# Expert feed-forward: the first product with its weights stationary and its tokens moving

## The chip, the cores and the metric

The kernel runs on one core of a Trainium2 chip. The metric is the device time of one execution in microseconds; less is better. The inputs are the seeded ones of the reference, and the whole computation is one launch.

## The reference, cut to what matters

Three parts follow each other. `_attn_ref` and `_moe_ref` give, for each of 8 × 576 tokens, a row `x` of 512 numbers. The change lies in the third part, a mixture of eight experts in which each token goes to one expert only (weights `w1` 8 × 512 × 1024, `w2` 8 × 1024 × 512):

```
def _moe2_ref(x, w_gate, w_local, w1, w2):
    ...
            e = ...                                  # the expert of this token
            p = np.exp(ls); p /= p.sum() + 1e-09     # softmax of the gate
            h = np.maximum(x[b, s] @ w1[e], 0.0)     # first product, 512 -> 1024
            out[b, s] = p[e] * (h @ w2[e])           # second product, 1024 -> 512
```

## The kernel before, in words

**Number format.** Every large product is done in f16 with each operand split in two: a high part and what the rounding left, the low part. `PASS = ((0, 0), (0, 1), (1, 0))` names the three partial products that are kept (high × high, high × low, low × high). So each product of a 128-row slice costs three matmuls.

**Stages.** Attention and the dense mix (`Mix.mm1` at L733 and `Mix.mm2` at L753) fill the first 1048 us of the profiled execution. Routing then sorts the tokens by expert into blocks of 128 tokens: 9 early blocks, and 34 from the second half of the routing. 41 of the 43 blocks are always computed; the last two stand behind a branch. The expert stage runs over these blocks, one after the other.

**One block of the expert stage.** `load_x(b)` gathers the 128 token rows (high and low part, 128 × 1024) by an indirect DMA on POOL's queue (L1069) and turns them by a DMA transpose on SP's queue (L1073) into `xt[b]`, 128 × 8 × 128: the features on the partitions, slices 0 to 3 the high part, 4 to 7 the low one. `load_w1` and `load_w2` (both through `weights`, L1083) fetch the split weights of the block's expert from DRAM into one of three buffers each, in four slices of 0.5 MB, on SP's queue; the DMA is skipped if the buffer holds that expert already (`cond=c`). `e1(b)` is the first product, for two groups `fg` of 512 hidden columns: 12 matmuls (4 slices of features × 3 passes) with the tokens stationary (128 × 128) and 512 columns of `w1` moving, into one PSUM bank `hp` (L1099). The result has the tokens on the partitions. ScalarE writes the high part of relu(hp) (L1106), VectorE the low part (L1107), both into the buffer `h` (tile `hb`, two buffers). The second product needs the hidden index on the partitions, so a DMA transpose on SP's queue (L1108) turns `h` into `ht` (tile `hx`, two buffers), one for each `fg`. `e2(b)` is the second product: 24 matmuls with `ht` stationary and 512 columns of `w2` moving (L1118), then a scaling by ScalarE (L1124) and an indirect DMA of the rows to the output on POOL's queue (L1125).

**Order.** The program text of the loop is `load_x(b + 3)`, `e1(b + 1)`, `e2(b)`. The weight loads for block b + 3 (`w1`) and b + 2 (`w2`) are issued inside the loops of `e1` and `e2`, one slice at a time, and `tick()` steps a list of background generators: in the first blocks these are the second half of the routing. A scheduler orders the instructions of each engine at build time by priority and its own estimate of when operands are there; on the chip each engine then takes its instructions in that fixed order. SP does no arithmetic: its queue carries, for each block, eight weight loads, two transposes of `h` and one transpose of `x`, in order.

Of the kernel before, what the change touches and what calls it, by code (L numbers as in the profile page):

```python
# [9 lines left out]
F16 = mybir.dt.float16  # L10
I32 = mybir.dt.int32
AF = mybir.ActivationFunctionType
ALU = mybir.AluOpType
# [12 lines left out]
RB = 3  # L26
# [135 lines left out]
PASS = ((0, 0), (0, 1), (1, 0))  # L162
# [16 lines left out]
def _build(tc, nc, ctx, A, stop):  # L179
# [517 lines left out]
    def tick(n=1.0):  # L697
        for it in list(bg):
            if it[0] is ew and phase[0] < EWS:
                continue  # L700
            it[1] += it[2] * n
            while it[1] >= 1.0:
                it[1] -= 1.0
                try:
                    next(it[0])
                except StopIteration:
                    bg.remove(it)
                    break
# [338 lines left out]
    M = {}  # L1047
# [14 lines left out]
    w1b, w2b = [], []  # L1062
    xg, xt, regs, hb = {}, {}, {}, {}
# [11 lines left out]
    def weights(b, dst, src, k0, k1):  # L1075

        if b not in regs:
            regs[b] = (nc.sync.value_load(ebi[0:1, 0, b:b + 1], min_val=0, max_val=NE - 1),
                       nc.sync.value_load(ebi[0:1, 1, b:b + 1], min_val=0, max_val=1))
        e, c = regs[b]  # L1080
        flat = dst[b % RB].rearrange("p c a n -> p (c a n)")
        cols = slice(2048 * k0, 2048 * k1)
        nc.sync.dma_start(flat[:, cols], src[bass.ds(e, 1), :, cols].rearrange("o p x -> p (o x)"), cond=c)  # L1083

    def load_w1(b, k0=0, k1=4):
        weights(b, w1b, WS1, k0, k1)

    def load_w2(b, k0=0, k1=4):
        weights(b, w2b, WS2, k0, k1)

    def e1(b, nxt=None):
        h = M["q"].tile([128, 2, 1024], F16, tag="hb", name=f"hb{b}", bufs=2)
        ht = M["q"].tile([128, 2, 8, 128], F16, tag="hx", name=f"hx{b}", bufs=2)
        for fg in range(2):
            hp = (psM, psO)[fg].tile([128, 512], F32, tag="ho"[fg], name=f"ehp{b}_{fg}")
            n = 0
            for c in range(4):
                for (x, y) in PASS:
                    nc.tensor.matmul(hp, xt[b][:, 4 * x + c], w1b[b % RB][:, 2 * c + fg, y],  # L1099
                                     start=n == 0, stop=n == 11)  # L1100
                    n += 1
                if c % 2 == 0 and nxt is not None:
                    load_w1(nxt, 2 * fg + c // 2, 2 * fg + c // 2 + 1)
                if c < 3:
                    tick()
            nc.scalar.activation(h[:, fg, :512], hp, AF.Relu)  # L1106
            nc.vector.scalar_tensor_tensor(h[:, fg, 512:], hp, 0.0, h[:, fg, :512], ALU.max, ALU.subtract)  # L1107
            nc.sync.dma_start_transpose(out=ht[:, fg], in_=h[:, fg])  # L1108
            tick()
        hb[b] = ht  # L1110

    def e2(b, nxt=None):
        h = hb.pop(b)
        op = psO.tile([128, 512], F32, tag="o", name=f"eo{b}")
        n = 0
        for f in range(8):
            for (x, y) in PASS:
                nc.tensor.matmul(op, h[:, f // 4, 4 * x + f % 4], w2b[b % RB][:, f, y], start=n == 0, stop=n == 23)  # L1118
                n += 1
            if f % 2 == 0 and nxt is not None:  # L1120
                load_w2(nxt, f // 2, f // 2 + 1)
            tick()
        ys = wp.tile([128, 512], F32, tag="U", name=f"ys{b}", bufs=8)
        nc.scalar.activation(ys, op, AF.Copy, scale=scl[:, b:b + 1])  # L1124
        nc.gpsimd.indirect_dma_start(out=A["out"], out_offset=bass.IndirectOffsetOnAxis(ap=sidx[:, b:b + 1], axis=0),  # L1125
                                     in_=ys, in_offset=None, bounds_check=NB * S - 1, oob_is_err=False)
# [61 lines left out]
    bg.append([r1, 0.0, R1_RATE])  # L1188
    load_w2(1)
    e1(0, 2)  # L1190
    last_sure = NBLK - NRARE

# [3 lines left out]
    for b in range(last_sure):  # L1196
        if b + RB == NEARLY:
            drain(r1)
        if sure(b + AHEAD) is not None:
            load_x(b + AHEAD)  # L1200
        if b + 1 < last_sure:
            e1(b + 1, sure(b + RB))
        e2(b, sure(b + RB - 1))
# [4 lines left out]
    def rare(b):  # L1208
        if b == NBLK:
            return  # L1210
        with tc.If(nused > b - NEARLY):
            load_x(b)
            load_w1(b)
            load_w2(b)
            e1(b)
            e2(b)
            rare(b + 1)
# [19 lines left out]
```

## Time and profile before

| | |
|---|---|
| median of 3 runs | 1526.61 us (1518.05 to 1538.52) |
| the profiled execution | 1531.01 us, span 1529.1 us, mean granted clock 0.966 |
| PE busy in the span | 1396.3 us (91%) |
| DVE, ACT, POOL busy | 769.7, 482.2, 335.8 us |
| expert stage, first e1 matmul to the end | 1048.6 to 1529.1 us |
| matmuls of e1 (L1099) and of e2 (L1118) | 984 each, 24 a block for 41 blocks |

PE is TensorE's matmuls and PEld its weight loads, which run beside them. A matmul's duration in the profile is its latency; matmuls overlap, so the time from one to the next is shorter than the duration. The granted clock is a share of 2.4 GHz; 1.0 is the upper level and 0.5 the lower one, 1.2 GHz. SPq is SP's queue, which issues DMAs.

### The profile page before, as it was taken

To read this page: it belongs to the slowest core of one execution; us is meant where nothing else is said; L and a number is where in the kernel's file an instruction comes from. 1 tells how busy PE (TensorE), PEld (TensorE's weight loads), DVE (VectorE), ACT (ScalarE), POOL (GpSimd) and SP (SyncE) were. 2 spreads that over 40 slices of the span, in tenths; PEclk is the share of its full clock that TensorE was granted. 3 is DMA by queue.
4 is the path that set the end of the run, shared out by engine and by line. 5 is a ranking of instruction groups with operands and counts; after the bars stand their busy time and mean duration, and the time that the engine had idled before them with its cause. 6 is when DMAs were issued, how large, how long until landed. Compare 5 with 4: busy or idle time off the path is not lost. (4 is left out here: it accounts for less than half of the span.)

```text
span 1529.1 us, 23161 instructions
## 1 busy us (share of the span) xinstructions
PE 1396.3 (91%) x8436; PEld 690.6 (45%) x8436; DVE 769.7 (50%) x1583; ACT 482.2 (32%) x892; POOL 335.8 (22%) x332
## 2 busy tenths in 40 slices
PE   3487899999999999999999999999899899989996
PEld 2233444534564454454444456454444344434442
DVE  6779967567555756666766765523611111111110
ACT  5355544344333434434434333111111111111111
POOL 4346423203200420320321220010112112111211
PEclk6698999999999999999999999999999999999998
DMA  8374465376466546547547355345968969897696
GB/s 266 80 228 144 146 180 164 97 219 171 122 155 166 186 120 200 151 134 208 148 131 208 104 139 152 96 160 168 288 133 191 236 139 226 201 324 147 131 206 161
DMA packets 319733, 260.82 MB, mean 171 GB/s; under 512 B 254784, under 2 KB 266176, under 8 KB 318977
## 3 DMA queue, kind: packets, MB, share of 16 engines
q1 hardware_dynamic: 313056, 239.13, 59.1%
q0 software_dynamic: 6560, 20.19, 4.4%
q8 instruction: 67, 1.10, 0.3%
q14 instruction: 50, 0.40, 0.1%
HBM read 267.38 MB, written 53.74 MB: 210 GB/s over the span
## 5 line engine op out<-in xcount | busy, mean ns | idle before, releaser
L753 PE MATMUL acc<-w2h,ht 128*128 128x512 f16 x1728 | 414.0, 382 | 0.8 <-DVE ul L761 0.8
L733 PE MATMUL hp<-ut,w1h 128*128 128x512 f16 x1536 | 376.5, 386 | 8.1 <-DMA ut<-unh 3.6
L733 PEld LDWEIGHTS <-w1h 128*128 128x128 f16 x1920 | 184.5, 99 | 194.9 <-issue 25.2
L753 PEld LDWEIGHTS <-ht 128*128 128x128 f16 x1728 | 166.6, 98 | 186.9 <-issue 10.4
L1118 PE MATMUL eo<-w2b,hx 128*128 128x512 f16 x984 | 229.7, 383 | 14.6 <-DMA hx<-hb 14.1
L1107 DVE SCALAR_TENSOR_TENSOR hb<-ehp,hb 128x512 f16<-128x512 f32 x82 | 56.7, 691 | 358.5 <-ACT hb L1106 326.4
L1099 PE MATMUL ehp<-w1b,xgt 128*128 128x512 f16 x984 | 229.5, 381 | 5.2 <-DMA w1b<-WS 3.4
L741 DVE SCALAR_TENSOR_TENSOR ht<-hp,ht 128x512 f16<-128x512 f32 (+1 forms) x160 | 101.4, 634 | 167.1 <-ACT ht L740 167.0
L1118 PEld LDWEIGHTS <-hx 128*128 128x128 f16 x984 | 96.0, 99 | 135.4 <-DMA hx<-hb 20.6
L1099 PEld LDWEIGHTS <-xgt 128*128 128x128 f16 x984 | 95.8, 98 | 121.6 <-issue 5.7
L260 ACT ACTIVATE so<-se 128x512 f16<-128x512 f32 x128 | 79.5, 628 | 181.9 <-DMA WS<-so 159.7
L740 ACT ACTIVATE ht<-hp 128x512 f16<-128x512 f32 (+1 forms) x160 | 87.4, 547 | 132.9 <-PE hp L733 127.4
L1125 POOL DMA_INDIRECT out<-ys,sidx x41 | 41.8, 1020 | 337.2 <-ACT ys L1124 332.4
L1124 ACT ACTIVATE ys<-eo,scl 128x512 f32<-128x512 f32 x41 | 28.2, 687 | 272.7 <-PE eo L1118 272.6
L346 POOL TENSOR_TENSOR qh<-q,qh 128x1420 f16<-128x1420 f32 x15 | 44.1, 2937 | 280.3 <-ACT qh L345 280.2
L261 DVE SCALAR_TENSOR_TENSOR so<-se,so 128x512 f16<-128x512 f32 x128 | 100.0, 790 | 10.3 <-ACT so L260 10.3
L1069 POOL DMA_INDIRECT xg<-XS,gidx x41 | 42.5, 1035 | 182.7 <-DVE sidx L1025 103.9
L1106 ACT ACTIVATE hb<-ehp 128x512 f16<-128x512 f32 x82 | 48.9, 597 | 105.6 <-PE ehp L1099 103.2
L370 PE MATMUL s<-k,p 64*32 64x288 f32 x256 | 24.8, 488 | 27.0 <-DVE ru L642 12.3
L733 PE MATMUL hp<-utr,w1h 128*128 128x256 f16 x384 | 47.1, 272 | 0.0
L557 PE MATMUL bp<-cst,eh 128*128 128x289 f16 (+1 forms) x192 | 33.0, 312 | 14.1 <-DVE g L472 5.9
L688 POOL TENSOR_TENSOR unh<-un,unh 128x512 f16<-128x512 f32 x32 | 38.6, 1214 | 30.6 <-ACT unh L687 30.6
(290 smaller groups left out, 1394.0 us busy)
## 6 DMA issues: line engine op xcount, KB each, us to landing
w1b<-WS SPq DMA_DIRECT2D x156, 512.0 KB
w2b<-WS SPq DMA_DIRECT2D x156, 512.0 KB
se<-in_w SPq DMA_DIRECT2D x64, 512.0 KB
WS<-so SPq DMA_DIRECT2D x128, 256.0 KB
sw<-in_wc SPq DMA_DIRECT2D x32, 512.0 KB
q<-in_qd SPq DMA_DIRECT2D x16, 710.0 KB
v<-in_vd SPq DMA_DIRECT2D x16, 640.0 KB
k<-in_kd SPq DMA_DIRECT2D x16, 576.0 KB
```

Source lines behind the costliest of these rows:

```text
L260: nc.scalar.activation(dst_hi, src, AF.Copy, scale=scale)
L261: nc.vector.scalar_tensor_tensor(dst_lo, src, scale, dst_hi, ALU.mult, ALU.subtract)
L346: nc.gpsimd.tensor_tensor(qh[:, 1], qt, qh[:, 0], op=ALU.subtract)
L733: nc.tensor.matmul(hp[:, :ntok], w1h[:, f, c, x], ut[:, 4 * y + c, :ntok], start=n == 0, stop=n == 11)
L740: nc.scalar.activation(ht[:, 0, :ntok], hp[:, :ntok], AF.Relu)
L741: pace[0] = nc.vector.scalar_tensor_tensor(ht[:, 1, :ntok], hp[:, :ntok], 0.0, ht[:, 0, :ntok], ALU.max, ALU.subtract).ins
L753: nc.tensor.matmul(self.acc[j], ht[:, x, 128 * j:128 * j + 128], w2h[:, f, y], start=f == 0 and n == 0, stop=f == 15 and n == 2)
L1069: nc.gpsimd.indirect_dma_start(out=g_, out_offset=None, in_=XS[0:rows], in_offset=bass.IndirectOffsetOnAxis(ap=gidx[:, b:b + 1], axis=0), ...
L1099: nc.tensor.matmul(hp, xt[b][:, 4 * x + c], w1b[b % RB][:, 2 * c + fg, y], start=n == 0, stop=n == 11)
L1106: nc.scalar.activation(h[:, fg, :512], hp, AF.Relu)
L1107: nc.vector.scalar_tensor_tensor(h[:, fg, 512:], hp, 0.0, h[:, fg, :512], ALU.max, ALU.subtract)
L1118: nc.tensor.matmul(op, h[:, f // 4, 4 * x + f % 4], w2b[b % RB][:, f, y], start=n == 0, stop=n == 23)
```

## The change

`e1` is turned around: the weights become the stationary operand, 128 hidden columns at a time, and the 128 tokens of the block move. A group `fg` is now four column blocks `f` of 12 matmuls each, 48 matmuls of 128 moving columns in place of 12 of 512; all four write their own 128 columns of the same PSUM bank. The result already has the hidden index on the partitions, so ScalarE and VectorE write the two parts straight into `ht`, and the DMA transposes of `h` and the buffer `hb` go. `hx` gets a third buffer. The weight loads and the calls of `tick()` stand at the same places of the loop, now counted by `f` in place of `c`. `e2` reads the same numbers from the new layout.

```diff
     def e1(b, nxt=None):
-        h = M["q"].tile([128, 2, 1024], F16, tag="hb", name=f"hb{b}", bufs=2)
-        ht = M["q"].tile([128, 2, 8, 128], F16, tag="hx", name=f"hx{b}", bufs=2)
+
+        ht = M["q"].tile([128, 2, 2, 512], F16, tag="hx", name=f"hx{b}", bufs=3)
         for fg in range(2):
             hp = (psM, psO)[fg].tile([128, 512], F32, tag="ho"[fg], name=f"ehp{b}_{fg}")
-            n = 0
-            for c in range(4):
-                for (x, y) in PASS:
-                    nc.tensor.matmul(hp, xt[b][:, 4 * x + c], w1b[b % RB][:, 2 * c + fg, y],
-                                     start=n == 0, stop=n == 11)
-                    n += 1
-                if c % 2 == 0 and nxt is not None:
-                    load_w1(nxt, 2 * fg + c // 2, 2 * fg + c // 2 + 1)
-                if c < 3:
+            for f in range(4):
+                n = 0
+                cols = slice(128 * f, 128 * f + 128)
+                for c in range(4):
+                    for (x, y) in PASS:
+                        nc.tensor.matmul(hp[:, cols], w1b[b % RB][:, 2 * c + fg, x, cols], xt[b][:, 4 * y + c],
+                                         start=n == 0, stop=n == 11, skip_group_check=True)
+                        n += 1
+                if f % 2 == 0 and nxt is not None:
+                    load_w1(nxt, 2 * fg + f // 2, 2 * fg + f // 2 + 1)
+                if f < 3:
                     tick()
-            nc.scalar.activation(h[:, fg, :512], hp, AF.Relu)
-            nc.vector.scalar_tensor_tensor(h[:, fg, 512:], hp, 0.0, h[:, fg, :512], ALU.max, ALU.subtract)
-            nc.sync.dma_start_transpose(out=ht[:, fg], in_=h[:, fg])
+            nc.scalar.activation(ht[:, fg, 0], hp, AF.Relu)
+            nc.vector.scalar_tensor_tensor(ht[:, fg, 1], hp, 0.0, ht[:, fg, 0], ALU.max, ALU.subtract)
             tick()
         hb[b] = ht
...
         for f in range(8):
             for (x, y) in PASS:
-                nc.tensor.matmul(op, h[:, f // 4, 4 * x + f % 4], w2b[b % RB][:, f, y], start=n == 0, stop=n == 23)
+                nc.tensor.matmul(op, h[:, f // 4, x, 128 * (f % 4):128 * (f % 4) + 128], w2b[b % RB][:, f, y],
+                                 start=n == 0, stop=n == 23)
                 n += 1
```

## Rows read from the trace of the kernel before

**Rows 1.** Windows of the expert stage: start:end, length, busy per engine, PEclk, DMA share, GB/s
```profile
1048.60:1112.00 63.40, 55.48 (x326) 29.19 (x325) 39.79 (x126) 10.99 (x19) 8.60 (x8) 0.97 0.99 283
1112.00:1340.00 228.00, 221.22 (x1016) 99.21 (x1015) 29.90 (x45) 39.42 (x64) 42.99 (x42) 0.99 0.82 188
1340.00:1406.00 66.00, 59.47 (x263) 25.28 (x262) 7.10 (x11) 9.21 (x15) 10.23 (x10) 0.97 0.93 243
1406.00:1490.00 84.00, 84.00 (x390) 38.04 (x389) 11.07 (x16) 14.73 (x24) 14.30 (x14) 1.00 0.75 164
1490.00:1518.00 28.00, 24.79 (x112) 10.52 (x110) 2.77 (x4) 4.37 (x7) 2.95 (x3) 1.00 0.95 221
```

**Rows 2.** Waits, 1048 to 1519 us: who waited for whom, us, times, longest
```profile
PE eo L1118 <- DMA hx<-hb: 14.1, 10, 2.7
...
PE ehp L1099 <- DMA w1b<-WS: 3.4, 4, 2.1
...
PE ehp L1099 <- DMA xgt<-xg: 1.8, 3, 1.4
```

**Rows 3.** Timeline of PE around stalls: start, length, instructions, [idle before]
```profile
1213.90 4.27 PE L1118 MATMUL eo<-w2b,hx 128*128 128x512 f16 x12 [2.69 <-DMA hx<-hb]
...
1351.73 0.81 PE L1099 MATMUL ehp<-w1b,xgt 128*128 128x512 f16 x3 [2.09 <-DMA w1b<-WS]
...
1354.33 4.03 PE L1118 MATMUL eo<-w2b,hx 128*128 128x512 f16 x12
```

**Rows 4.** Timeline of PE, one undisturbed block apart
```profile
1246.49 2.75 PE L1118 MATMUL eo<-w2b,hx 128*128 128x512 f16 x12
...
1256.85 2.75 PE L1118 MATMUL eo<-w2b,hx 128*128 128x512 f16 x12
```

**Rows 5.** Instructions of four lines: duration in ns, min/median/max, first to last start
```profile
L1099 PE MATMUL ehp<-w1b,xgt x984: 376/379/634, 1048.6 to 1506.7; 128*128 128x512 f16 x197
...
L733 PE MATMUL hp<-utr,w1h x384: 269/273/273, 423.6 to 953.7; 128*128 128x256 f16 x192
...
L485 PE MATMUL s<-pth,qh x540: 189/193/261, 29.1 to 847.0; 128*128 128x64 f16 x180
...
L429 PE MATMUL pps<-vhl,et x450: 216/219/316, 19.1 to 832.5; 128*64 128x128 f16 x150
```

**Rows 6.** Timeline of PE: runs of short matmuls in earlier stages
```profile
427.45 1.47 PE L733 MATMUL hp<-utr,w1h 128*128 128x256 f16 x12
...
846.33 0.83 PE L485 MATMUL s<-pth,qh 128*128 128x64 f16 x23
...
831.78 0.89 PE L429 MATMUL pps<-vhl,et 128*64 128x128 f16 x26
...
833.27 0.17 PE L770 MATMUL lp<-wgh,xt 128*128 128x18 f16 x1
...
833.45 0.17 PE L772 MATMUL lp<-wgh,xt 128*128 128x9 f16 x1
```

**Rows 7.** SP's issue of the two transposes of a block, ns min/median/max
```profile
L1108 SPq DMA_TRANSPOSE hx<-hb x82: 971/1257/3911, 1056.3 to 1508.5; - x82
...
L1073 SPq DMA_TRANSPOSE xgt<-xg x41: 962/1242/6377, 1023.3 to 1481.2; - x41
```

**Rows 8.** Waits of SP's own queue, 1048 to 1519 us
```profile
SPq L1108 <- DVE hb L1107: 21.0, 21, 2.4
```

**Rows 9.** Groups of instructions by line: count | busy us, mean ns | idle before
```profile
L1107 DVE SCALAR_TENSOR_TENSOR hb<-ehp,hb 128x512 f16<-128x512 f32 x82 | 56.7, 691 | 358.5 <-ACT hb L1106 326.4 <-DMA hx<-hb 14.2 <-DMA xgt<-xg 7.1
L1106 ACT ACTIVATE hb<-ehp 128x512 f16<-128x512 f32 x82 | 48.9, 597 | 105.6 <-PE ehp L1099 103.2 <-issue 2.0 <-DMA hx<-hb 0.4
```

**Rows 10.** Page: span and instructions; DMA queue of instruction blocks (packets, MB, share)
```profile
span 1529.1 us, 23161 instructions
...
q8 instruction: 67, 1.10, 0.3%
```

**Rows 11.** Window with the densest matmuls of the earlier stages, columns as in Rows 1
```profile
230.00:250.00 20.00, 20.00 (x197) 10.86 (x195) 12.25 (x25) 8.32 (x14) 7.89 (x8) 1.00 0.63 185
```

## The prediction, made before the changed kernel was run

> **What bounds the kernel now.** I read the windows first, since only the expert stage is edited. From its first e1 matmul at 1048.6 us to the last e2 matmul at about 1518 us it lasts 469.4 us, and PE is busy 55.5 + 221.2 + 59.5 + 84.0 + 24.8 = 445.0 us of it [rows 1]. So PE bounds the stage, and 24.4 us of idle time are all that any better supply of PE could give. The windows also show where it lies: none between 1406 and 1490 us, where the DMA engines are busy 0.75 of the time, and 17.6 of the 24.4 us in the three windows in which that share is 0.93 to 0.99.
>
> The waits name it next [rows 2]. PE stood 14.1 us, in ten pieces, for the transposes of h, 3.4 us for w1 and 1.8 us for the tokens' transposes, seven pieces together. The remaining 5.1 us (24.4 − 19.3) I put down to the routing in the first blocks, which the change does not touch.
>
> Then the timeline, for what a stall costs beyond its length [rows 3]. After the wait of 2.69 us the next 12 matmuls took 4.27 us where an undisturbed dozen takes 2.75 [rows 4]: the clock had dropped to its lower level, at a price of 1.5 us. Soon after the w1 wait of 2.09 us a dozen took 4.03 us, 1.3 us too long. Each stall also drains the pipeline: the matmul before it counts its whole 379 ns [rows 5] and not the 215.5 ns by which matmuls follow each other, so 0.16 us.
>
> **What e1 costs on PE.** In an undisturbed dozen the spacing is (2.75 − 0.379) / 11 = 215.5 ns [rows 4, 5]. A block of 48 matmuls takes 1256.85 − 1246.49 = 10.36 us, 215.8 ns each, so nothing else is in it [rows 4]. Half of a block, 24 × 215.5 = 5.17 us, is e1.
>
> After the change e1 is 96 matmuls of 128 moving columns, each with its own 128 × 128 weight load. The trace has no such run, so I take the spacing from its neighbours on both sides, all with a load for every matmul. At 256 columns it is (1.47 − 0.273) / 11 = 108.8 ns; at 64 columns (0.83 − 0.193) / 22 = 29.0 ns [rows 5, 6]. With 215.5 ns at 512 all three are the column count at 2.4 GHz plus 2.1 to 2.3 ns, so 128 columns give 53.3 + 2.3 = 55.6 ns. The nearest row by column count, 128 columns against stationary tiles of 64 columns, runs in pairs that share the array: (0.89 − 0.219) / 25 = 26.8 ns a matmul, 53.7 ns a pair with two loads [rows 5, 6]. That is the low end. For the high end I add the whole load: eight matmuls of 18 and 9 columns start within 833.45 − 833.27 = 0.18 us, 25.7 ns each [rows 6], which bounds what a full load needs from below its cover; were none of it hidden, 128 columns would take 55.6 + 25.7 = 81 ns. I take 55.6, because the 64-column row is decisive: its 29.0 ns leave no room for a load of 25 ns after 26.7 ns of columns, so loads do run beside the matmul before them.
>
> Here the Trainium skill speaks against the change: "TensorE: Matmul & The Clock Gate", section "Back-to-back issue gap", says that a stream of load and matmul pairs keeps about 81 ns a matmul at 128 columns, and 131 ns at 512. By it e1 would take 96 × 81 = 7.8 us a block. The trace disagrees with its second figure (215.5 ns here at 512), and no run here shows the first.
>
> With 55.6 ns e1 takes 5.34 us a block, +0.17 us, and over 41 blocks **+6.8 us** (−0.7 us at 53.7 ns, +107 us at 81 ns; a load half hidden, 68 ns, +56 us).
>
> **What goes.** The 14.1 us for h, ten drains of 0.16 us and the 1.5 us of low clock: **−17.2 us**. In its place e2's loads wait for VectorE, 0.60 + 0.69 us after the last e1 matmul of a group [rows 9]. Between e1(b) and e2(b) stands e1(b + 1), 5.3 us of PE work, so this costs nothing; without that cover it would be 1.3 us a block. The last block is covered by e2 of the block before. ScalarE and VectorE do the same instructions on the same shapes, 1.2 and 1.4 us of a block of 10.4, so they stay off the path.
>
> **What is late next.** With h's transposes gone, w1 and the tokens' transposes decide: 5.2 us of waits, seven drains (1.1) and 1.3 us of low clock, 7.6 us. Two things pull them down. Two of the three transposes of a block leave the DMA engines, which are busy most in the windows with stalls [rows 1, 7]. And SP loses 82 issues of 1.26 us [rows 7] and 21.0 us in which it stood for VectorE [rows 8] with the next weight slices queued behind it, so w1 and w2 slices start up to 2.5 us and a wait sooner. One thing pulls the other way: the first twelve matmuls now need all four w1 slices within 0.67 us, where the old order met them over 2.6 us. In the four w1 waits this can add up to 2 us each, 8 us. Bounds −7.6 and +8; I take −4, since both windows with w1 waits had a saturated DMA which loses most of its transposes. The extra hx buffer and the loss of hb cost nothing: ScalarE and VectorE waited 0.4 and 14.2 us for h's transposes [rows 9], both far from the path.
>
> **Sum.** Against the profiled execution: 1531.0 + 6.8 − 17.2 − 4.0 = 1516.6 us, −0.9%. That execution lies 4.4 us above the median of the three runs, 1526.6; taken from the median the same change gives 1512.2. I predict **1515 us**.
>
> **Rivals.**
> *A: other transfers take over the stalls.* The hx waits lie where DMA is saturated, so they may have been the queue and not the transposes: e2 and e1 then wait for w1, w2 and x instead. For it: shares of 0.93 to 0.99 [rows 1], and e1's new haste for four slices. Against it: two thirds of the stage's steady transposes leave. If half of the 17.2 us comes back and w1 costs 4 us more, it is 1531 + 6.8 − 8.6 + 4 = 1533 us, no change, or 1529 from the median.
> *B: the weight load is not hidden*, in e1's runs of 96. It decides above 5.17 + 21.2 / 41 = 5.69 us a block, 59.3 ns a matmul; from there the kernel is slower than before. At 81 ns it is 1531 + 107 − 21 = 1617 us, 6% slower. For it: the weights come from a buffer that DMAs fill meanwhile, and no run here lasts as long. Against it: the 29.0 ns. The skill's 81 ns are this rival's case; the row at 64 columns contradicts their mechanism.
> *C: instructions arrive too slowly.* PE takes 240 instructions a block in place of 96, 5,904 more in all. With 1.10 MB for 23,161 instructions, 47 bytes each, in packets of 1.10 MB / 67 = 16.4 KB [rows 10], these are 17 packets more. If each cost what the worst stall did, 2.69 us and 1.5 us of low clock, that is +71 us, 1588 us; with a quarter of them 1534. Against it: 197 matmuls, each with a load, went through in 20 us with PE never idle [rows 11], 9.9 a microsecond; the change wants 120 in 10.5 us, 11.4.
>
> **How the numbers follow.** Forecast 0.67; A 0.15; B 0.07; C 0.04; 0.04 that more goes than is shown idle here, 0.03 for anything slower that I do not see. The forecast's own range is 1502 (everything above gone, the low end of the spacing, from the median) to 1527. The range stretches to A: **1502 to 1533**. I call 2% (30.5 us) what tells a change from none. Faster than 1496 needs more than the 25 us that PE loses to DMA in all: 0.05. Slower than 1557 is B, part of C and of the rest: 0.10. Within: 0.85.
>
> **What would show it.** In the trace after: L1099 with 3,936 matmuls of 128 columns whose runs of 12 start 0.66 to 0.68 us apart; no L1108; PE idle in the expert stage near 6 us; DMA share below 0.7 in the windows from 1112 to 1490 us; an undisturbed block of 10.5 us. The prediction is wrong if that block is above 10.9 us (B), if PE's waits name w1b, w2b or xgt with over 12 us (A), or if PE idles on "issue" at regular distances (C).

## The result, and the profile after

The changed kernel takes 1513.86 us (median of 14 runs, 1508.12 to 1520.39) against 1527.19 us before (14 runs). The ratio is 0.991, with a 95% interval of 0.9889 to 0.993: faster, the interval is clear of 1, but by less than the 2% that I had called the line. 1515 us was predicted, 1502 to 1533 the range.

The profiled execution took 1512.5 us, its span is 1510.6. The windows of its expert stage (columns as in [rows 1]):

```profile
1051.16:1112.00 60.84, 56.64 (x697) 45.37 (x696) 40.82 (x128) 11.48 (x20) 10.76 (x8) 1.00 0.96 260
1112.00:1340.00 228.00, 228.00 (x2606) 167.02 (x2604) 29.05 (x42) 40.79 (x65) 44.95 (x44) 1.00 0.63 174
1340.00:1406.00 66.00, 66.00 (x755) 48.30 (x753) 9.55 (x14) 11.88 (x19) 12.26 (x12) 1.00 0.43 116
1406.00:1490.00 84.00, 84.00 (x960) 61.48 (x959) 10.75 (x17) 15.05 (x24) 12.16 (x12) 1.00 0.56 147
```

PE is busy without a gap from 1112 to 1490 us, at the upper level of the clock. The DMA share fell from 0.82 to 0.63, from 0.93 to 0.43 and from 0.75 to 0.56 in the same three windows [rows 1]. What is left of PE's waits, 1040 to 1515 us, in answer to [rows 2]:

```profile
PE lp L770 <- DMA xt<-xh: 2.0, 1, 2.0
...
PE ehp L1101 <- DMA w1b<-WS: 1.3, 1, 1.3
```

A block in the timeline of PE, and e1's durations, in answer to [rows 4, 5]:

```profile
1204.35 5.34 PE L1119 MATMUL eo<-w2b,hx 128*128 128x512 f16 x24
1209.53 5.52 PE L1101 MATMUL ehp<-xgt,w1b 128*128 128x128 f16 x96
1214.89 5.34 PE L1119 MATMUL eo<-w2b,hx 128*128 128x512 f16 x24
```

```profile
L1101 PE MATMUL ehp<-xgt,w1b x3936: 216/219/230, 1051.2 to 1488.9; 128*128 128x128 f16 x197
```

A block is 1214.89 − 1204.35 = 10.54 us. The spacing of the short matmuls is (5.52 − 0.219) / 95 = 55.8 ns, so 96 of them cost 5.36 us, and the 41 blocks lose (10.54 − 10.36) × 41 = 7.4 us. The stage, from the first e1 matmul to the end of the last e2 matmul, went from 469.4 us to 448.3 (1051.16 to 1499.45): 21.1 us less. The part before it, which the edit does not touch, was 2.6 us longer in this execution. The stage's length is read from one execution of each run.

### The profile page after: what moved, and what is told of

It is laid out like the page before. It is cut to its first block, busy times and chain, and to the rows that moved or that the text cites. A ratio compares the mean times of both kernels' runs of the same rounds, so it can differ in the third digit from the quotient of the medians.

```text
span 1510.6 us, 29008 instructions
## 1 busy us (share of the span) xinstructions
PE 1395.1 (92%) x11388; PEld 812.8 (54%) x11388; DVE 768.4 (51%) x1583; ACT 482.9 (32%) x892; POOL 337.1 (22%) x332
## 5 line engine op out<-in xcount | busy, mean ns | idle before, releaser
L1101 PE MATMUL ehp<-xgt,w1b 128*128 128x128 f16 x3936 | 229.3, 219 | 1.3 <-DMA w1b<-WS 1.3
L1101 PEld LDWEIGHTS <-w1b 128*128 128x128 f16 x3936 | 224.1, 98 | 11.2 <-DMA w1b<-WS 1.5
L1109 DVE SCALAR_TENSOR_TENSOR hx<-ehp,hx 128x512 f16<-128x512 f32 x82 | 56.7, 691 | 335.8 <-ACT hx L1108 335.7
L1119 PE MATMUL eo<-w2b,hx 128*128 128x512 f16 x984 | 219.2, 379 | 0.0
L1108 ACT ACTIVATE hx<-ehp 128x512 f16<-128x512 f32 x82 | 48.9, 597 | 179.0 <-PE ehp L1101 179.0
```

The source lines that it names most:

```text
L1101: nc.tensor.matmul(hp[:, cols], w1b[b % RB][:, 2 * c + fg, x, cols], xt[b][:, 4 * y + c], start=n == 0, stop=n == 11, skip_group_check=True)
L1108: nc.scalar.activation(ht[:, fg, 0], hp, AF.Relu)
L1109: nc.vector.scalar_tensor_tensor(ht[:, fg, 1], hp, 0.0, ht[:, fg, 0], ALU.max, ALU.subtract)
L1119: nc.tensor.matmul(op, h[:, f // 4, x, 128 * (f % 4):128 * (f % 4) + 128], w2b[b % RB][:, f, y], start=n == 0, stop=n == 23)
```

## The experiments

The changed kernel was also run beside the first group of experiments. The three groups ran on three chips, and its ratio to the kernel before was 0.991 in the result and 0.995 in group 1, so comparisons of times stay inside a group as far as they can (groups 2 and 3 have no run of the changed kernel itself), and the rows carry what the times cannot.

| run | median, us | ratio [95%] | PE's waits for h, w1, w2, x, us | expert stage, us |
|---|---|---|---|---|
| before, as profiled | | | 19.3 | 469.4 |
| after, as profiled | 1513.86 | 0.991 [0.9889, 0.993] | 1.3 | 448.3 |
| after_again (group 1) | 1519.03 | 0.995 [0.9929, 0.9971] | 2.8 | 456.0 |
| direct (1) | 1500.66 | 0.9842 [0.9809, 0.9875] | 0.8 | 438.5 |
| late (1) | 1532.77 | 1.0053 [1.0033, 1.0072] | 26.0 | 476.7 |
| ghost (1) | 1543.4 | 1.0113 [1.0079, 1.0148] | 20.7 | 481.9 |
| g_small (2) | 1522.39 | 0.9965 [0.9939, 0.999] | 4.6 | 459.2 |
| g_nowait (2) | 1529.74 | 1.0 [0.9976, 1.0024] | 9.9 | 469.3 |
| g_copy (2) | 1521.57 | 0.9955 [0.9931, 0.9979] | 3.8 | 457.7 |
| c_outer (2) | 1515.74 | 0.9907 [0.9875, 0.994] | 0 | 454.8 |
| c_outer2 (3) | 1512.59 | 0.9903 [0.9871, 0.9935] | 0 | 448.1 |
| hx2 (3) | 1514.58 | 0.99 [0.9876, 0.9924] | 1.7 | 449.3 |

The medians of the kernel before were 1525.31, 1528.1 and 1529.28 us in the three groups.

**after_again**, no edit.

> The changed kernel as it stands, beside the next three on the same chip. All theories: 1514 us, ratio to the kernel before 0.991, an undisturbed block of 10.54 us.

1519.03 us, 0.995: the same kernel gains 6.3 us here, not 13.3, and the two intervals hardly touch. An undisturbed block is 10.54 us, as expected; the first blocks were not. The window from 1050 to 1112 us has a granted clock of 0.94: after two waits for w1 near 1098 us PE went at the lower level from 1098.8 to 1105.6 us (granted clock 0.50), and the stage was 456.0 us. More than half of the later blocks are disturbed too: they take 10.61 us at the median, because e1 stops for up to 0.3 us about three quarters through. One such e1:

```profile
1205.63 5.60 PE L1101 MATMUL ehp<-xgt,w1b 128*128 128x128 f16 x96
```

It took 5.52 us in the first trace. No DMA and no engine is named for these short stops. They stand in the traces of groups 1 and 2 with 96 short matmuls a block, and not in the result's nor in group 3's.

**direct**: the old e1, no transposes.

```diff
-            nc.sync.dma_start_transpose(out=ht[:, fg], in_=h[:, fg])
...
-        hb[b] = ht
+        hb[b] = h
...
-                nc.tensor.matmul(op, h[:, f // 4, 4 * x + f % 4], w2b[b % RB][:, f, y], ...)
+                nc.tensor.matmul(op, h[:, f // 4, 512 * x + 128 * (f % 4):512 * x + 128 * (f % 4) + 128], w2b[b % RB][:, f, y], ...)
```

> The kernel before with the transposes of h left out: e2 takes the untransposed h as its stationary operand, so the turn of h is missing from the computation; e1 keeps its 24 matmuls of 512 columns. My theory (the transposes' wait is the gain, the 96 short matmuls are a cost of 55.8 - 215.5/4 = 1.9 ns each, 7.4 us in all): 1514 - 7.4 = about 1506 us, block 10.36 us. Rival (the new form costs nothing by itself, or helps by its order): the same time as the changed kernel, 1514 us.

Its median is 18.4 us below the changed kernel's, not 7.4. Its timeline of PE gives the block that was expected, 1215.69 − 1205.33 = 10.36 us:

```profile
1205.33 5.34 PE L1116 MATMUL eo<-w2b,hb 128*128 128x512 f16 x24
...
1215.69 5.34 PE L1116 MATMUL eo<-w2b,hb 128*128 128x512 f16 x24
```

So 7.4 us of the distance are the short matmuls. The stage of direct is 9.8 us shorter than that of the changed kernel as first profiled and 17.5 us shorter than after_again's; what goes beyond 7.4 lies mostly in the first five blocks (60.3 us in direct, 63.5 and 68.8 in the two traces of the changed kernel), where the changed kernel waits for w1 and direct hardly does, and in after_again's short stops.

**late**: the old kernel with more time for its transposes.

```diff
-        ht = M["q"].tile([128, 2, 8, 128], F16, tag="hx", name=f"hx{b}", bufs=2)
+        ht = M["q"].tile([128, 2, 8, 128], F16, tag="hx", name=f"hx{b}", bufs=3)
...
+            h = M["q"].tile([128, 1024], F16, tag="hb", name=f"hb{b}_{fg}", bufs=2)
...
-        e2(b, sure(b + RB - 1))
+        if b:
+            e2(b - 1, sure(b + RB - 2))
+    e2(last_sure - 1)
```

> The kernel before with every transpose kept, but e2 one block later (e1(b+1), then e2(b-1)), so that about 15 us lie between a transpose and its reader in place of 5. My theory (latency of the transposes under a busy DMA): PE's waits for hx fall from 14.1 us to under 2 us, the waits for w1 and x (5.2 us) stay or grow to 8 us, PE block 10.36 us: 1527 - 17 + 0 to 3 = 1510 to 1513 us, no slower than the changed kernel. Rival A (the DMA engines' capacity is what is short, and stalls move to w1, w2 and x): waits for weights of 12 us or more, 1520 us or above.

My theory failed here. Waits of PE in this run, 1040 to 1545 us:

```profile
PE eo L1118 <- DMA w2b<-WS: 12.6, 11, 3.0
PE ehp L1098 <- DMA w1b<-WS: 11.3, 8, 4.1
PE eo L1118 <- DMA hx<-hb: 2.1, 1, 2.1
```

The wait for h went as intended, from 14.1 to 2.1 us, and 23.9 us of waits for weights stand in its place; [rows 2] had 3.4 for w1 and none for w2. The kernel became slower than before. One thing beside the order was changed: `h` now has two buffers of half a block in place of two of a whole block, and ScalarE stood 72.2 us for h's transposes, against 0.4 before [rows 9]. PE's waits do not name ScalarE, but the run does not part this from the DMA engines' load.

**ghost**: the changed kernel, with the transposes' work put back and nobody waiting for it.

```diff
             nc.vector.scalar_tensor_tensor(ht[:, fg, 1], hp, 0.0, ht[:, fg, 0], ALU.max, ALU.subtract)
+            gh = M["q"].tile([128, 8, 128], F16, tag="gh", name=f"gh{b}_{fg}", bufs=2)
+            nc.sync.dma_start_transpose(out=gh, in_=ht[:, fg].rearrange("p a n -> p (a n)"))
```

> The changed kernel with the 82 transposes put back as idle work: ht is turned into a tile that nothing reads. SP and the DMA engines carry what they carried before, only nobody waits for it. My theory: no hx wait returns; waits for w1 and x return up to the 7.6 us that I had priced, so 1514 + 0 to 8 us, 1514 to 1522 us, DMA share in 1112 to 1340 us back at about 0.8. Rival A (load, not latency): most of the 25 us comes back as waits for w1, w2 and x, 1530 us or above.

1543.4 us, 24 us above the changed kernel and 18 above the old one. Waits of PE, then of SP:

```profile
PE ehp L1101 <- DMA w1b<-WS: 18.6, 13, 3.6
...
PE ehp L1101 <- DMA xgt<-xg: 1.6, 2, 0.9
```

```profile
SPq L1111 <- DVE hx L1109: 29.0, 27, 3.0
```

So the transposes cost PE time although nothing reads them. The waits for w1 fall where the DMA engines are full: from 1096 to 1105 us, where PE was busy 3.05 of 9 us, the share is 1.14 (it adds up the times of packets, which can overlap), from 1355 to 1361 us, 2.47 of 6 us, it is 1.00. Three runs part their two effects, SP's wait with weight loads queued behind it and the work on the DMA engines. Each changes the second added line of ghost:

```diff
 g_small
+            nc.sync.dma_start_transpose(out=gh[:, 0:1], in_=ht[:, fg, 1, 384:])
 g_nowait
+            nc.sync.dma_start_transpose(out=gh, in_=xt[b].rearrange("p a n -> p (a n)"))
 g_copy
+            nc.sync.dma_start(gh.rearrange("p a n -> p (a n)"), ht[:, fg].rearrange("p a n -> p (a n)"))
```

> The changed kernel with 82 idle transposes of one eighth of the size (128 x 128) at the places and with the waits for VectorE that the transposes of h had on SP's queue. If the idle transposes of the ghost run cost 24 us because SP stood for VectorE with weight loads queued behind (29 us of such waits there): at least half comes back, ratio to the kernel before 1.002 or above. If the volume on the DMA engines was the cause: the changed kernel's time or up to 4 us more, ratio 0.993 to 0.998, waits for w1 under 6 us.

> The changed kernel with 82 idle transposes of full size at the same places, but of the block's tokens xt, which landed long before, so that SP never stands for VectorE there. Volume theory: the ghost run's time again, ratio 1.005 to 1.013, waits for w1 of 12 us or more. Queue theory: the changed kernel's time, ratio 0.993 to 0.999.

> The changed kernel with 82 plain copies of ht (256 KB each, rows of 2 KB) in place of the idle transposes, at the same places and with the same waits for VectorE. If a transpose costs the DMA engines by its 256-byte packets (1,024 of them), the copy of the same bytes costs well under half of the ghost run's 24 us: ratio 0.994 to 1.002. If bytes or the place on the queue decide: the ghost run's time, ratio 1.008 or above.

The window from 1112 to 1340 us of ghost, g_small, g_nowait and g_copy, each from its own trace (columns as in [rows 1]; the changed kernel has 0.63 there):

```profile
1112.00:1340.00 228.00, 224.28 (x2512) 163.66 (x2509) 35.31 (x63) 39.42 (x63) 41.27 (x41) 1.00 0.82 183
```

```profile
1112.00:1340.00 228.00, 227.54 (x2550) 164.84 (x2549) 30.63 (x49) 40.10 (x64) 42.88 (x42) 1.00 0.63 160
```

```profile
1112.00:1340.00 228.00, 227.18 (x2560) 166.78 (x2559) 36.11 (x66) 39.52 (x63) 42.00 (x42) 1.00 0.89 191
```

```profile
1112.00:1340.00 228.00, 227.86 (x2576) 166.66 (x2574) 33.78 (x58) 40.11 (x64) 42.90 (x42) 1.00 0.72 203
```

The share is the last figure but one. SP's waits in g_small, then PE's in g_nowait:

```profile
SPq L1111 <- DVE hx L1109: 25.4, 19, 3.9
```

```profile
PE ehp L1101 <- DMA w1b<-WS: 9.0, 6, 3.0
```

SP stood for VectorE 25.4 us in g_small and 56.2 us in g_copy, against 29.0 in ghost, and PE waited 4.6 and 3.8 us: SP's wait alone does little. The time that SP spends on issuing does not explain ghost either: an idle transpose takes SP 1.12 us at the median in g_small, 1.26 in ghost and 1.27 in g_nowait. The full transposes without that wait bring 9.9 us of PE's waits and the time of the old kernel, so alone the volume costs more than SP's wait does. But the volume theory had wanted a ratio of 1.005 to 1.013 and 12 us of waits for w1; 1.0 and 9.0 came, between the two theories. A copy of the same bytes does not bring it. Its window moves more (203 GB/s) at a smaller share (0.72) than the transposes' (191 GB/s at 0.89). Both effects together, in ghost, cost about twice what the volume does alone (20.7 against 9.9 us of waits), though the mean share from 1112 to 1340 us is lower there (0.82 against 0.89); ghost ran in group 1, the other three in group 2. So the volume and SP's wait work together; how, and what share of ghost's loss belongs to each, stays open.

**c_outer and c_outer2**: w1's slices met one after the other again.

```diff
-            for f in range(4):
-                n = 0
-                cols = slice(128 * f, 128 * f + 128)
-                for c in range(4):
-                    for (x, y) in PASS:
+            n = 0
+            for c in range(4):
+                for (x, y) in PASS:
+                    for f in range(4):
+                        cols = slice(128 * f, 128 * f + 128)
                         nc.tensor.matmul(hp[:, cols], ...,
-                                     start=n == 0, stop=n == 11, skip_group_check=True)
+                                     start=n == 0 and f == 0, stop=n == 11, skip_group_check=True)   # c_outer2; c_outer: n == 0
```

> The changed kernel with e1's loops turned: feature slice c outside, column block f inside, four accumulations open in one bank, so that w1's four slices are met over 2.7 us as before the change and not within 0.67 us. My theory (the new form's haste for four slices costs the 1.3 to 2.8 us of w1 waits and the slow clock behind them): w1 waits under 1 us, 2 to 6 us below the changed kernel, ratio 0.988 to 0.992. Rival (the first blocks are bound by weight loads in any order): the same time as the changed kernel, ratio 0.993 or 0.994.

In c_outer each of the four start flags also resets the other three sums of the bank, so the kernel leaves out the first product of three column blocks; the time is that of the order.

> The c_outer order with one start flag for the bank instead of four (only the first matmul of a group clears it), so that all sums are kept. Feature slice c outside, column block f inside. If w1's haste was part of what the changed kernel still loses: no waits for w1, ratio to the kernel before 0.988 to 0.992. Rival: 0.993 or 0.994, as the changed kernel.

No wait for w1 is left in either trace, where the changed kernel has 1.3, 2.8 and, in hx2, 1.7 us. In its place PE waits 1.0 and 1.1 us for VectorE in the routing near 1095 us, a wait that the other three do not have, so little is won. The median of c_outer2 is 2.0 us below hx2's in the same group, the ratio is the same (0.9903 and 0.99). The five traces speak for the haste for four slices; the times cannot tell. c_outer's stage is 6.7 us longer than c_outer2's: 3.9 us of this lie in the first five blocks, and the rest goes with short stops in e1 like those of after_again (block 10.60 us at the median, 10.54 in c_outer2).

**hx2**: two hx buffers.

```diff
-        ht = M["q"].tile([128, 2, 2, 512], F16, tag="hx", name=f"hx{b}", bufs=3)
+        ht = M["q"].tile([128, 2, 2, 512], F16, tag="hx", name=f"hx{b}", bufs=2)
```

> The changed kernel with two hx buffers in place of three. My step that the third buffer costs and gives nothing: 0.991 to 0.995, the changed kernel's ratio. Rival (ScalarE's write of ht(b+2) must wait for e2(b), which e1(b+1) delays): PE or ScalarE waits for hx, 0.997 or above.

The ratio is 0.99, and neither PE nor ScalarE waits for hx: the third buffer does nothing.

**cols64 and cols32**: e1's matmuls cut further (one execution each).

```diff
+                        for t in range(0, 128, 64):   # cols32: 32
-                        nc.tensor.matmul(hp[:, cols], w1b[b % RB][:, 2 * c + fg, x, cols], xt[b][:, 4 * y + c], ...
+                            nc.tensor.matmul(hp[:, 128 * f + t:128 * f + t + 64], w1b[b % RB][:, 2 * c + fg, x, cols],
+                                             xt[b][:, 4 * y + c, t:t + 64], start=n == 0 and t == 0, ...
```

> The changed kernel with every e1 matmul cut in two of 64 moving columns, each with its own load: 192 a block. If the spacing is columns / 2.4 GHz + 2.3 ns and the load is hidden: 29.0 ns, e1 5.57 us, block 10.75 us, +9 us on the changed kernel. If instructions come too slowly at 34 matmuls with loads in a microsecond, kept up for 5.6 us: block 11.5 us or more, PE idle on issue.

> The changed kernel with 384 e1 matmuls of 32 moving columns a block. If a matmul with its load cannot follow the last in less than the 25.7 ns of the 18- and 9-column run: e1 9.9 us, block 15.0 us, +185 us. If only columns count: 15.6 ns, block 11.2 us, +26 us.

Timeline of PE in cols64:

```profile
1209.00 5.34 PE L1121 MATMUL eo<-w2b,hx 128*128 128x512 f16 x24
1214.18 5.76 PE L1102 MATMUL ehp<-xgt,w1b 128*128 128x64 f16 x192
1219.78 5.34 PE L1121 MATMUL eo<-w2b,hx 128*128 128x512 f16 x24
```

and in cols32, with the waits that PE had there below it:

```profile
1207.81 5.00 PE L1102 MATMUL ehp<-xgt,w1b 128*128 128x32 f16 x194
```

```profile
PE ehp L1102 <- issue: 51.5, 44, 4.1
```

At 64 columns the block is 10.78 us, for 10.75 expected, and the spacing (5.76 − 0.193) / 191 = 29.1 ns. The single run took 1536.74 us, more than the 9 us added: its stage began 5 us late and PE stood 4.9 us on issue, in six pieces. At 32 columns the spacing is (5.00 − 0.176) / 193 = 25.0 ns, for a floor of 25.7 expected, but the run took 1748.51 us: beside the floor PE stood 51.5 us on issue, 44 times in 41 blocks. The trace tells what it stood for: each of the 44 waits ended 1.2 to 1.6 us after a packet of 16,384 bytes on the queue of instruction blocks had landed, and so did the five long ones of cols64 after 1180 us (1.3 to 1.4 us). There were 183 such packets in cols32, 91 in the changed kernel and 67 before it [rows 10].

## Why the prediction was right, point by point

**The short matmuls.** 55.6 ns a matmul and +6.8 us were forecast from the rows at 64 and 256 columns; 55.8 ns and +7.4 us came. The load is hidden, and rival B is out: cols64 and cols32 put its floor at 25.0 ns a pair, less than half of what 128 columns take.
The Trainium skill, "TensorE: Matmul & The Clock Gate", section "Back-to-back issue gap", has 81 ns for this stream and would have made e1 7.8 us; the 55.8 ns decide against it. The same page, "Wait — 56ns, not 53.3ns?", gives columns / 2.4 GHz + 2.5 ns and a least distance of about 25 ns, and with both the traces agree.

**What goes.** −17.2 us for the waits for h, with their drains and slow clock: all of them went, and in the profiled execution e2 never waits for VectorE or ScalarE, as forecast.

**What is late next.** −4 us was taken between −7.6 and +8. In the profiled pair the waits for w1 and x fell from 5.2 to 1.3 us, one for xt in the routing grew from 0.7 to 2.0, and the clock stood at its upper level in all windows, so this step gave more than I took: of 21.1 us that the stage lost net, 17.2 − 7.4 = 9.8 are h and the spacing, and some 11 are the rest. Of these the step's own terms are 6.2: 3.9 us of waits, 1.0 of drains and 1.3 of slow clock. Some 4 lie in the routing of the first blocks, which the prediction had put at nothing: PE's other waits there fell from 5.1 to 2.9 us, and a third stretch at the lower level of the clock, which the sum did not hold, is gone in this execution. It stands in the trace of the kernel before, and 3.4 us at half the clock cost at most 1.7 us:

```profile
1090.70:1094.10 3.40, 3.40 (x9) 1.09 (x9) 3.30 (x15) 0.00 (x0) 0.00 (x0) 0.50 1.09 348
```

In the medians, 13.3 us net, the step gave about 3.5, close to the −4; in group 1, where the same kernel gained 6.3 us, it cost about 3.5. So the closeness of 1513.86 to 1515 is in part luck: the −4 was met in one group of runs and missed in the other.

**Small slips of the sums.** The ends of the forecast's own range, 1502 and 1527, come out as 1501 and, from the profiled execution, 1529 when its terms are added. Rival C's 17 more instruction packets were 24 (67 before, 91 after). Neither changes the forecast.

**The reason behind it was half wrong.** The sum priced the waits for h as a term of its own, which goes when "the transposes of h" go; the late and ghost runs were built on reading it as their latency. Both missed their times. With the transposes kept and read later, PE waited for the weights instead; with the transposes kept and read by nobody, it did so too. What these runs point to is the DMA engines' time in the stretches where their share is near 1, together with SP's queue. h was only what the program asked for last. Rival A had this mechanism right ("they may have been the queue and not the transposes"), and was wrong about the outcome, because the change takes the load away together with the wait. The prediction had named that too, two of the three transposes of a block leaving, but gave it to the −4 alone. An edit that had only hidden the wait, as late does, would have been forecast at 1510 to 1513 us and came out at 1532.77.

**Rival C.** At the changed kernel's 11.4 matmuls a microsecond PE did not stand on issue in the profiled execution. At 192 and 384 e1 matmuls a block it did, 4.9 and 51.5 us, and the waits ended shortly after instruction packets landed: the mechanism is real. Where it begins is not settled. The sign that the prediction gave for C, PE idle on issue at regular distances, shows in small at this change's own rate: the short stops of after_again come about once a block and make the blocks from the sixth to the end 2.5 us longer than in the first trace (387.3 against 384.8 us). They do not follow the landing of an instruction packet at a fixed distance, as those of cols32 do, and their cause stays open.

**Best version.** c_outer2 has the shortest stage of the complete kernels (448.1 us) and no waits for w1; its 1512.59 us are not told apart from the changed kernel. direct shows what a transpose-free result at 512 moving columns would be worth, 18.4 us in group 1, and cannot be had, since it leaves out the turn.

## What to carry to other kernels

A wait names what came last, not what is short. Before pricing it as latency, look at the share of the shared resource in the same stretch: where that was near 1 here, hiding the wait moved it to the weights, and taking the work away removed it. Putting the suspected work back with nobody reading it showed in one run that the work itself costs time; which property of it, size, kind or place in the queue, took three more and is not wholly settled.

The price of a matmul shape that a trace does not hold can be read from two shapes that it holds, one shorter and one longer, if both load new weights every time.

## What the runs showed of the hardware that was not expected

A transpose of 256 KB costs the DMA engines far more than a copy of 256 KB: from 1112 to 1340 us the share went from 0.63 to 0.89 with two full transposes a block (g_nowait; 0.82 in ghost) and to 0.72 with two copies.

PE took a matmul and its load every 25.0 ns for some 5 us in cols32, but with 384 of them a block it stood on issue 44 times for up to 4.1 us, at a DMA share of 0.34 from 1112 to 1340 us. Every one of these waits ended 1.2 to 1.6 us after a 16,384-byte packet of instructions had landed.

A start flag in one quarter of the 512 columns of a PSUM bank makes the next matmul in the other quarters overwrite and not add. The Trainium skill, "PSUM — Partial Sum Buffer", section "The four PSUM rules", says so and gives the one-flag form; c_outer2, with one flag, keeps all sums. Which products c_outer leaves out follows from the rule and is read from no row.
